# Attention outputs turned in 32x32 blocks by VectorE, with `w_in`'s rows loaded to match; batch 0's first layer in four parts of 128 tokens; four column tiles to a PSUM bank

## The chip, the core and the metric

The kernel runs on one core of a Trainium2 chip. Its engines are TensorE (PE, with its weight loads shown apart as PEld), VectorE (DVE), ScalarE (ACT), GpSimd (POOL, which also issues the DMAs that convert types) and SyncE (SP, which here only issues DMAs). The metric is the device time of one execution in microseconds. Before the change it is 340.51 us, the median of three runs (339.76 to 341.34).

## What is computed

Eight batches of global-local attention with 8 heads of 64: 32 global queries attend to all 544 keys, and 512 local queries attend to the 32 global keys and to the local keys at most 32 positions away. The 8 x 544 rows of 512 outputs then go through two layers with a gate between them. Inputs and output are float32; the kernel computes in float16 and sums in float32.

```python
s_g = scale * np.matmul(q_g, k_all.transpose(0, 1, 3, 2))
out_g = np.matmul(sm(s_g), v_all)
s_ll = np.where(np.abs(pos[:, None] - pos[None, :]) <= 32, scale * np.matmul(q_l, k_l.transpose(0, 1, 3, 2)), -1e9)
s_l = np.concatenate([scale * np.matmul(q_l, k_g.transpose(0, 1, 3, 2)), s_ll], axis=-1)
out_l = np.matmul(sm(s_l), np.concatenate([v_g, v_l], axis=2))
x = concatenate([out_g, out_l], axis=2).transpose(0, 2, 1, 3).reshape(8 * 544, 512)
h = x @ w_in                     # 512 -> 2048
g = h * np.clip(h + 3, 0, 6) / 6
out = g @ w_out                  # 2048 -> 512
```

## The kernel before, in words

**Order of work.** The program is not written in the order in which it runs. Each step is an `Op` with its engine (or a choice of two), an expected cost, the steps it depends on, the buffers it takes and the buffers it reads. The steps stand in streams (`s` scores, `mx` mask and maximum, `ex` exponentials, `t` turned probabilities, `av` values, `nm` normalisation, `xp` turned outputs, `mf` first layer, `t1` and `gate` its gate, `ms` second layer, and so on), each stream with a rank. `Plan.lay` (L118) picks the next step again and again: the one that can start first by its own clock, and within 0.03 us of that the one with the lowest rank. Costs, ranks and the constants `SPARE` and `ALONE` of `Plan` therefore decide the order on each engine, and that order is then fixed: each engine runs its instructions in it, waiting for what they need. `SPARE` is what DVE's finish must be ahead of ACT's for a copy that either may do. `ALONE` decides whether PE may enter an operation on part of its array when only one such operation is ready.

**Local attention** (`local`, L603). The 512 local tokens of a batch are 16 blocks of 32. Step `n` of four handles a pair of blocks `2n`, `2n+1` of each half of the sequence (`f` is the half). Scores (L624 for batches 2 to 7, L637 for batches 0 and 1, which arrive as 32-bit words) go to PSUM tiles `s`, for half of batch 0's pairs to `m`; DVE adds the mask and takes the maximum (L664); ACT takes the exponential (L670); PE turns the eight 128x128 blocks of probabilities (L679) into the PSUM tile `t`; ACT or DVE copies them to `et` (L308 and L310, the two sides of `either`, L303); PE multiplies by the values (L693, 64 small matmuls into the tile `a`); DVE takes the reciprocal of the sums and normalises to `x` (L701, L702). Then four PE matmuls with the identity turn `x` (L715), again into `t` (for batch 0 into `t` or `m`), and ACT or DVE copies the result to `xt` (stream `xpc`), where a partition is one of 128 rows of `w_in`.

**Global attention** (`globe`, L723) does the same in two steps `s` of four heads each: scores (L735, L743), maximum (L751 for each half, L752), exponentials (L757, L758), turning (L768), values (L777), normalisation (L785, L786); after the second, PE turns both (L792) and a copy puts them into `xg`, which collects the global rows of all batches.

**Layers.** `first` (L813) makes one column tile of 128 of the 2048 hidden columns: four matmuls over the 512 inputs (L821) into one PSUM tile `m` of three, then ACT makes `t1` (L833) and DVE the gate (L828), which writes `gts`. `moe_first` (L868) calls it for 16 column tiles; for batch 0 twice, each time for half of the tokens. `second` (L838) makes 128 rows of the output: 16 matmuls (L850), a copy to `ot` (L858 or L860) and a store from SP. `moe_global` (L891) does both layers for the 256 global rows. The first layer of a batch needs `xt` of all its pairs (of batch 0's half, of its two pairs). The scores of batch `b` are held until the first layer of batch `b-1` has come to a set point (`hold`).

**Loads.** POOL issues all loads from the inputs in a fixed order: batch 0's `q`, `k`, `v`, then eight loads of `w_in` (L505, a quarter of the rows by half of the columns, at most three under way), batch 1, four loads of `w_out` (L513), then the later batches. SP copies `rawq`, `rawk` and `vg` within the chip's memory for later batches and issues the stores. Batch 0 handles its pairs in the order 1, 0, 2, 3.

Of the kernel before, what the change touches and what calls it, by code (L numbers as in the profile page):

```python
# [37 lines left out]
class Plan:  # L38
# [6 lines left out]
    SWITCH, ALONE = 0.097, 0.0  # L45
    SPARE, PHASES = 0.3, 9
# [137 lines left out]
def kernel(  # L184
# [33 lines left out]
    AHEAD = 3  # L218
    HALVES = 1
# [22 lines left out]
    for c in range(NDFF):  # L242
        sizes[f"gts{c}"] = 2
# [34 lines left out]
    gts = [tiles(f"gts{r}_", NDFF, [P, Sl], FP16) for r in range(2)]  # L278

    mps = tiles("m", 3, [P, 512], FP32, pp)  # L280
    sps = tiles("s", 2, [P, 512], FP32, pp)
# [4 lines left out]
    for name, rank in (("l0", 0), ("ld", 5), ("lq", -2), ("sh", 0), ("sq", 0), ("st", 2), ("g0", 0), ("ga", -9), ("first", -9), ("gc", -3), ("msk", 1), ("tq", lambda n: 0 if n < 5 else 3), ("kg", 0.5), ("vs", 1.5), ("clr", 1),  # L286
                       ("s", -1), ("mx", lambda n: 1.2 if n < 33 else 2.7), ("ex", 1.2), ("t", -0.5), ("etc", 0), ("av", 0), ("nm", 0),
                       ("xp", -1.2), ("xpc", 0), ("gx", 1), ("gxc", 1),
                       ("mf", lambda n: 9 + n * 1e-3), ("ms", lambda n: 9 + (n + 2 * NDFF + 2) * 1e-3), ("t1", 0), ("gate", -1.4), ("ot", 1.5)):
        plan.stream(name, rank)  # L290
# [161 lines left out]
    def vg_load(b, to):  # L452

        st = state[b]
        v = st["v"] = Buf("v", NI // 2 + 2)
# [42 lines left out]
    def load_w_in():  # L498
        n = dff // 2
        rows = moe_w_in.rearrange("(k a e d) c -> a k d e c", k=2, a=2, e=2)  # L500
        got = []
        for i in range(2):
            for k in range(2):
                for a in range(2):
                    got.append(load("l0", "POOL", 0.65, 1.4, w_in_t[i][a * D:(a + 1) * D, 2 * k:2 * k + 2],  # L505
                                    rows[a, k, :, :, i * n:(i + 1) * n], got[-AHEAD:][:1] if len(got) >= AHEAD else ()))
# [96 lines left out]
    def local(b, n, spare, halves=False):  # L603
# [8 lines left out]
        def scored(r):  # L612
            return mps[ps[r].slot] if spare else sps[r]
# [69 lines left out]
        def summed(t):  # L683

            return aps[t.slot][:, :, 0:NC * D1].rearrange("p u (c d) -> p u c d", c=NC)

        def values():
            o = summed(av)
            for un, i in enumerate(pair):
                for c in range(NC):  # L690
                    for e in range(2):
                        for f in range(2):
                            nc.tensor.matmul(out=o[quarter(e, f), un, c, 0:D + 1],  # L693
                                             lhsT=ets[et.slot][:, un, c, quarter(e, f) if b >= WORDS else quarter(e ^ (c // 2), f)],
                                             rhs=vs[v.slot][:, i % NU, (i + NI * f) // NU, 2 * c + e, 0:D + 1])
# [281 lines left out]
```

## Time and profile before

| | us |
|---|---|
| median of three runs | 340.51 |
| profiled execution | 340.96 |
| span of its instructions | 339.2 |
| PE busy (share) | 313.6 (92%) |
| DVE busy | 257.0 (76%) |
| ACT busy | 234.1 (69%) |
| POOL busy | 156.2 (46%) |
| granted PE clock, mean | 0.983 |

The profile is of one execution. A row of a group of instructions gives line, engine, operation, output<-input by the names in the program, and the shapes; behind the bar busy time and the mean of one in ns; then the idle time ahead of them and what ended it. A row of the timeline or of the chain of waits begins with the start in us and the length. Instructions of one engine overlap at their ends, so a group that runs without a pause takes less than its count times the mean; what one costs in such a stretch is the distance from start to start.

### The profile page before, as it was taken

What the parts mean: (1) busy time and instruction counts of PE and PEld (TensorE: products, weight loads), DVE (VectorE), ACT (ScalarE), POOL (GpSimd) and SP (SyncE); (2) the same over time, 40 slices, a digit from 0 to 9 for tenths busy, and PEclk for the clock granted to TensorE, in tenths of its full rate; (3) what the DMA queues carried; (4) which work ended last, traced back from release to release, by engine and by line L of the source; (5) the groups of instructions that cost most, each with busy time, mean ns of one, the idle gap of its engine ahead of it and who ended that gap; (6) DMA issues with size and microseconds to landing.
All of it is one profiled execution on the core that took longest, in us unless ns stands there. A gap on an engine that the chain in (4) does not pass through costs nothing.

```text
span 339.2 us, 11248 instructions
## 1 busy us (share of the span) xinstructions
PE 313.6 (92%) x4456; PEld 169.5 (50%) x4456; DVE 257.0 (76%) x952; ACT 234.1 (69%) x576; POOL 156.2 (46%) x195
## 2 busy tenths in 40 slices
PE   0648879899999999999999999999999999999996
PEld 0536656454455455544554555454545544445654
DVE  5887997678988799989998999899969844433310
ACT  4778778555888697679867784799699644443431
POOL 8899589108961982694359258756000000000000
PEclk9976999999999999999999999999999999999999
DMA  8989999979960996999679948991000000010103
GB/s 131 185 154 165 185 227 164 177 204 147 221 124 35 154 206 86 91 153 179 145 99 150 169 90 80 183 174 41 31 33 34 35 32 33 31 60 34 62 34 92
DMA packets 107076, 39.27 MB, mean 116 GB/s; under 512 B 92368, under 2 KB 100816, under 8 KB 107024
## 3 DMA queue, kind: packets, MB, share of 16 engines
q0 software_dynamic: 93536, 17.44, 64.6%
q1 hardware_dynamic: 12912, 20.99, 22.7%
q8 instruction: 35, 0.57, 0.7%
q10 hardware_dynamic: 576, 0.13, 0.2%
q14 instruction: 17, 0.14, 0.1%
HBM read 35.39 MB, written 8.91 MB: 131 GB/s over the span
## 4 chain that ended last, share of the span: by engine, by line
PE 87%; DVE 7%; issue 2%; POOL 1%; ACT 1%; POOLq 0%; ACTq 0%
PE m L850 36%; PE m L821 33%; PE t L679 5%; PE a L693 3%; PE s L624 2%; PE t L715 2%; DVE gts L828 1%; PE t L768 1%; PE s L735 1%; PE s L637 1%; PE a L777 1%; DVE sm L664 1%; POOL wout L298 1%; DVE kt L534 1%; DVE qt L529 1%
## 5 line engine op out<-in xcount | busy, mean ns | idle before, releaser
L850 PE MATMUL m<-wout,gts 128*128 128x512 f16 (+1 forms) x560 | 135.1, 373 | 0.0
L828 DVE SCALAR_TENSOR_TENSOR gts<-t,m 128x512 f16<-128x512 f32 (+1 forms) x160 | 95.2, 602 | 46.1 <-ACT t L833 45.0
L821 PE MATMUL m<-xt,win 128*128 128x512 f16 (+1 forms) x576 | 126.9, 359 | 3.0 <-DVE gts L828 1.9
L833 ACT ACTIVATE t<-m 128x512 f32<-128x512 f32 (+1 forms) x160 | 84.3, 532 | 44.6 <-PE m L821 41.2
L486 POOL COPY vs<-v 32x1056 f32<-32x1056 f32 (+3 forms) x81 | 78.2, 966 | 34.9 <-DMA v<-in_v_l_dram 30.1
L670 ACT ACTIVATE ex<-sm,mx 128x128 f16<-128x128 f32 x256 | 86.1, 394 | 8.4 <-DVE mx L664 7.9
L821 PEld LDWEIGHTS <-win 128*128 128x128 f16 x640 | 59.9, 99 | 54.3 <-issue 4.2
L850 PEld LDWEIGHTS <-gts 128*128 128x128 f16 x560 | 51.1, 98 | 48.5 <-issue 0.7
L664 DVE CUSTOM_DVE_ANT_0 sm<-s,mask 128x128 f32<-128x128 f32 x240 | 56.9, 285 | 5.9 <-PE s L624 2.9
L858 ACT COPY ot<-m 128x512 f32<-128x512 f32 (+1 forms) x34 | 19.5, 573 | 16.9 <-PE m L850 16.2
L298 POOL DMA_DIRECT2D rawq<-in_q_l_dram x12 | 12.6, 1057 | 36.2 <-DMA vs<-vg 16.3
L298 POOL DMA_DIRECT2D v<-in_v_l_dram x32 | 28.2, 905 | 0.0
L702 DVE TENSOR_TENSOR x<-a,rec 128x512 f16<-128x512 f32 x32 | 22.1, 692 | 1.1
L664 DVE DVE_READ_ACCUMULATOR2_ANT mx<- 128x1 f32 x256 | 21.3, 83 | 0.0
L679 PE MATMUL t<-ident,ex 128*128 128x128 f16 x256 | 20.9, 228 | 0.0
L679 PEld LDWEIGHTS <-ex 128*128 128x128 f16 x256 | 17.2, 102 | 5.5 <-issue 0.7
L637 PE MATMUL s<-kt,qt 32*32 32x128 f16 x384 | 7.0, 246 | 12.3 <-DVE kt L542 10.0
L571 DVE STREAM_TRANSPOSE qt<-rawq 128x512 f16<-128x512 f16 x24 | 15.9, 692 | 0.0
L575 DVE STREAM_TRANSPOSE kt<-rawk 128x512 f16<-128x512 f16 x24 | 15.8, 687 | 0.0
L308 ACT COPY et<-t 128x1024 f16<-128x1024 f16 x13 | 13.1, 1010 | 3.5 <-PE t L679 3.4
L637 PEld LDWEIGHTS <-qt 32*32 32x32 f16 x512 | 6.5, 102 | 17.7 <-issue 9.6
L310 DVE COPY et<-t 128x1024 f16<-128x1024 f16 x19 | 13.0, 685 | 3.0 <-PE a L693 2.6
(95 smaller groups left out, 262.7 us busy)
## 6 DMA issues: line engine op xcount, KB each, us to landing
out_dram<-ot SPq DMA_DIRECT2D x31, 256.0 KB, 2.1
vs<-vg SPq DMA_DIRECT2D x32, 132.0 KB, 5.8
v<-in_v_l_dram POOLq DMA_DIRECT2D x32, 128.0 KB, 6.5
rawq<-in_q_l_dram POOLq DMA_DIRECT2D x12, 256.0 KB, 5.8
rawk<-in_k_l_dram POOLq DMA_DIRECT2D x12, 256.0 KB, 7.2
rawq<-rawq SPq DMA_DIRECT2D x12, 254.0 KB, 5.6
rawk<-rawk SPq DMA_DIRECT2D x12, 254.0 KB, 5.7
win<-in_moe_w_in_dram POOLq DMA_DIRECT2D x8, 256.0 KB, 6.2
```

The source lines that it names most:

```text
L298: eng.dma_start(out=o() if callable(o) else o, in_=i() if callable(i) else i)
L486: (nc.gpsimd if op.engine == "POOL" else nc.vector).tensor_copy(out=o(), in_=i())
L637: nc.tensor.matmul(out=scored(r)[quarter(e ^ r, f), z:z + P], lhsT=pairs(qt[k.slot])[rows, c, i * W:(i + 1) * W, bb], rhs=pairs(kt[k.slot] ...
L664: nc.vector.tensor_tensor_reduce(out=sms[sm.slot], in0=scored(c // 2)[:, z:z + P], in1=masks[:, m, :], scale=-scale, scalar=3.0e38, op0=AL ...
L670: nc.scalar.activation(out=exs[ex.slot][:, un, c, :], in_=sms[sm.slot], func=EXP, scale=-1.0, bias=mxs[mx.slot])
L679: nc.tensor.matmul(out=turned(tp)[:, z:z + P], lhsT=exs[ex.slot][:, un, c, :], rhs=ident, is_transpose=True)
L702: nc.vector.tensor_tensor(out=xs[x.slot], in0=o[:, :, :, 0:D], in1=recs[rec.slot].to_broadcast([P, 2, NC, D]), op=ALU.mult)
L821: nc.tensor.matmul(out=o if len(x.shape) == 2 else o.rearrange("p (a c) -> p a c", a=2), lhsT=w_in_t[c // 8][:, m, (c % 8) * P:(c % 8 + 1) ...
L828: nc.vector.scalar_tensor_tensor(out=g, in0=shape(t1s[t1.slot][:, 0:n]), scalar=1.0, in1=shape(mps[ps.slot][:, 0:n]), op0=ALU.min, op1=ALU ...
L833: r = plan.add("t1", Op(("ACT", 0.09 + n * 0.00083), lambda: nc.scalar.activation(out=t1s[t1.slot][:, 0:n], in_=mps[ps.slot][:, 0:n], func ...
L850: nc.tensor.matmul(out=mps[ps.slot][:, 0:n], lhsT=gfn(c), rhs=w_out_t[c // 4][:, c % 4, cols], start=(c == 0), stop=(c == NDFF - 1))
L858: nc.scalar.copy(out=o, in_=i)
```

## The change

- `xturn` is one DVE transpose of `x` for each pair, in 32x32 blocks, straight into `xt`. Such a transpose exchanges partition and column only within a block. So the values are summed in another place: partition `32*(h % 4)` + token, and the free dimension holds half, unit and `h // 4`. After the transpose a partition is `32*(h % 4) + d % 32` and one of four slots is `2*(h // 4) + d // 32`. `load_w_in` loads `w_in`'s rows in that order. The columns of `xt` are now pair, half, unit, token, so 128 output rows are two pieces of 64, stored by two DMAs.
- The global rows go the same way: both steps' values are one `av` step (`globe_values`), one normalisation, one DVE transpose into `xg`. The maximum of both halves is one reduction over a PSUM tile of two banks; the two `s` tiles become one of `[P, 2, 512]`.
- `first` takes several column tiles: their matmuls go to one PSUM tile `m` and have one `t1` and one gate. Batch 0 goes through the first layer in four parts of 128 tokens with four column tiles each, in the order of pairs 1, 0, 2, 3; the global rows in two column tiles of 256. `gts` tiles hold four column tiles.
- Constants and ranks of the planner change: `ALONE` 0.0 to 1.0, `SPARE` 0.3 to 0.6, ranks of `s`, `etc`, `xp`, `vs`, `st`.

```diff
-    SWITCH, ALONE = 0.097, 0.0
-    SPARE, PHASES = 0.3, 9
+    SWITCH, ALONE = 0.097, 1.0
+    SPARE, PHASES = 0.6, 9
...
+    PARTS, CG = 4, 4
...
-    gts = [tiles(f"gts{r}_", NDFF, [P, Sl], FP16) for r in range(2)]
+    gts = [tiles(f"gts{r}_", NDFF // CG, [P, CG, Sl], FP16) for r in range(2)]
...
-    sps = tiles("s", 2, [P, 512], FP32, pp)
+    sps = tiles("s", 1, [P, 2, 512], FP32, pp)[0]
...
-        rows = moe_w_in.rearrange("(k a e d) c -> a k d e c", k=2, a=2, e=2)
+        rows = moe_w_in.rearrange("(k h a d) c -> k a h d c", k=2, h=4, a=2)
...
-                    got.append(load("l0", "POOL", 0.65, 1.4, w_in_t[i][a * D:(a + 1) * D, 2 * k:2 * k + 2],
-                                    rows[a, k, :, :, i * n:(i + 1) * n], got[-AHEAD:][:1] if len(got) >= AHEAD else ()))
+                    got.append(load("l0", "POOL", 0.65, 1.4, w_in_t[i][:, 2 * k + a], rows[k, a, :, :, i * n:(i + 1) * n],
+                                    got[-AHEAD:][:1] if len(got) >= AHEAD else ()))
...
-                            nc.tensor.matmul(out=o[quarter(e, f), un, c, 0:D + 1],
+                            nc.tensor.matmul(out=o[hq * W:(hq + 1) * W, f, 2 * un + kh, 0:D + 1],
...
-            st["xt"] = Buf("xt", NDFF * (2 if b == 0 else 1))
+            st["xt"] = Buf("xt", NDFF * (PARTS if b == 0 else 1))
...
         def xturn():
-            o = turned(xp)[:, 0:4 * P].rearrange("d (k z n q) -> d k z n q", k=2, z=NU, n=2)
-            for un in range(2):
-                for kk in range(2):
-                    nc.tensor.matmul(out=o[:, kk, :, un, :], lhsT=xs[x.slot][:, un, 2 * kk:2 * kk + 2].rearrange("p a d -> p (a d)"),
-                                     rhs=ident, is_transpose=True)
-        a = plan.add("xp", Op(("PE", 0.24), xturn, done, [xp], [x], lat=0.25, n=8))
-        st["xT", n] = either(
-            "xpc", 0.5, 0.36,
-            lambda: xts[xt.slot].rearrange("d k (f t) -> d k f t", f=2)[:, :, :, 2 * n * W:(2 * n + 2) * W],
-            lambda: turned(xp)[:, 0:4 * P].rearrange("d (k f t) -> d k f t", k=KC, f=2), [a], new, [xp])
+
+            nc.vector.transpose(out=xts[xt.slot][:, :, n * P:(n + 1) * P].rearrange("p k (t q) -> p t k q", q=W),
+                                in_=xs[x.slot].rearrange("p f (u k) (a q) -> p (f u) (k a) q", u=2, a=2))
+        st["xT", n] = plan.add("xp", Op(("DVE", 0.7), xturn, done, new, [x]))
...
         def top():
-            for f in range(2):
-                nc.vector.tensor_reduce(out=tops[mx.slot][:, f:f + 1], in_=sps[f][:, 0:N1].rearrange("q (a c) -> q a c", a=1), axis=AX, op=ALU.max)
+            nc.vector.tensor_reduce(out=tops[mx.slot][:, 0:1], in_=sps[:, :, 0:N1], axis=AX, op=ALU.max)
...
+    def globe_values(b):
...
+        a = plan.add("av", Op(("PE", 0.48), lambda: [f(av) for f, _, _ in both], [c for _, c, _ in both] + [st["g4"]] + st["v0"],
+                              [av], [et for _, _, et in both] + [v], lat=0.3, n=80, mode=("tall", "tall")))
...
+        st["xg"] = plan.add("gx", Op(("DVE", 0.22), lambda: nc.vector.transpose(
+            out=xg[:, :, b * Sg:(b + 1) * Sg], in_=xgns[xgn.slot].rearrange("p k (a q) -> p (k a) q", q=W)), [n], (), [xgn]))
...
-    def first(xfn, n, gfn, deps, takes, reads):
+    def first(xfn, n, cs, gfn, deps, takes, reads):
...
+        all_ = n * len(cs)
...
+        a = [paced(Op(("PE", 4 * n * 0.000423 + (0.02 if n < 256 else 0.0)), lambda k=k, c=c: mm(k, c), deps + w_in_l[c // 8], [] if k else [ps], reads, lat=0.25, n=8), n / Sl / NDFF)
+             for k, c in enumerate(cs)]
...
-        parts = 2 if b == 0 else 1
+        parts = PARTS if b == 0 else 1
...
+        for at, h in enumerate((1, 0, 2, 3) if parts == 4 else range(parts)):
+            deps = [st["xT", i] for i in range(h * per, (h + 1) * per)]
...
-        second(lambda c: gts[st["gts"][c].slot][c][:, j * P:(j + 1) * P], lambda c: [st["gts"][c]], lambda c: st["gd"][c],
-               [(out[row:row + P, :], 0, P)], parts)
+        rows = out[b * S + Sg:(b + 1) * S].rearrange("(f r) d -> f r d", f=2)
+        second(lambda c: gts[st["gts"][c // CG].slot][c // CG][:, c % CG, j * P:(j + 1) * P], lambda c: [st["gts"][c // CG]], lambda c: st["gd"][c],
+               [(rows[f, j * P // 2:(j + 1) * P // 2], f * P // 2, P // 2) for f in range(2)], parts)
```

## What was predicted, before the changed kernel had run

> **What bounds the kernel now.** I read the chain of waits first, then stretches of the span engine by engine.
>
> ```profile
> PE 87%; DVE 7%; issue 2%; POOL 1%; ACT 1%; POOLq 0%; ACTq 0%
> PE m L850 36%; PE m L821 33%; PE t L679 5%; PE a L693 3%; PE s L624 2%; PE t L715 2%; DVE gts L828 1%; PE t L768 1%; PE s L735 1%; PE s L637 1%; PE a L777 1%; DVE sm L664 1%; POOL wout L298 1%; DVE kt L534 1%; DVE qt L529 1%
> ...
> 0.00:30.00 30.00, 13.12 (x379) 9.94 (x380) 21.70 (x104) 20.57 (x63) 26.70 (x56) 0.84 1.09 155
> 30.00:55.00 25.00, 20.68 (x419) 15.58 (x423) 22.32 (x84) 19.64 (x58) 19.77 (x23) 0.98 1.52 197
> 55.00:75.00 20.00, 18.84 (x411) 10.61 (x399) 13.58 (x58) 12.45 (x35) 5.79 (x7) 1.00 1.54 180
> 75.00:270.00 195.00, 195.00 (x2873) 98.80 (x2871) 177.42 (x667) 154.45 (x371) 103.95 (x111) 1.00 0.97 117
> 270.00:336.00 66.00, 65.96 (x397) 34.56 (x395) 22.00 (x42) 26.67 (x52) 0.00 (x0) 1.00 0.13 45
> ```
>
> The columns of the stretches are length, then busy us of PE, PE's weight loads, DVE, ACT and POOL, then granted clock, DMA share and GB/s. The reader is to see two regimes. Up to 55 us PE is busy for 33.8 of 55; DVE and ACT, working through batch 0's attention and gates, fill much of the rest. From 75 to 336 PE is never idle. But a busy PE need not be a fast one, so I look at how closely its operations follow each other.
>
> ```profile
> 55.54 0.82 PE L850 MATMUL m<-wout,gts 128*128 128x512 f16 x3
> 74.87 1.89 PE L821 MATMUL m<-xt,win 128*128 128x512 f16 x8
> 100.65 0.39 PE L715 MATMUL t<-ident,x 128*128 128x128 f16 x4
> 100.88 1.89 PE L850 MATMUL m<-wout,gts 128*128 128x512 f16 x8
> 102.70 0.43 PE L735 MATMUL s<-kt,qg 64*32 64x288 f16 x8
> 103.06 0.62 PE L679 MATMUL t<-ident,ex 128*128 128x128 f16 x8
> 103.51 1.89 PE L850 MATMUL m<-wout,gts 128*128 128x512 f16 x8
> ...
> 15.68 0.97 PE t L679 x8
> 53.63 1.31 PE m L821 x12
> 279.80 0.86 PE m L850 x4
> ```
>
> From start to start: eight transposes at 103.06 take 0.45 us, 56 ns each; twelve 256-column matmuls 1.31 us, 109 ns each; four 512-column ones 0.86 us, 216 ns each. Eight 512-column matmuls ahead of a score (100.88 to 102.70) take 1.82 us, 0.09 more than 8 x 0.216: that is the price of entering an operation on part of the array. With these prices over all 4456 matmuls, PE's own work is about 303 us. Compared with the start of each matmul, 31.5 us had been lost by 74.87, and only another 1.1 by PE's last matmul. So behind 75 us a microsecond of PE work removed is a microsecond of the end, as long as its feeders keep up. Ahead of 55 us PE work is nearly free, and what counts is when the second layer (L850) of batch 0 can begin.
>
> **The change, part by part.** *1. Turned outputs leave PE.*
>
> ```profile
> L715 PE MATMUL t<-ident,x 128*128 128x128 f16 x120 | 11.6, 219 | 0.4 <-DVE x L702 0.3
> L715 PE MATMUL m<-ident,x 128*128 128x128 f16 x8 | 1.2, 307 | 2.2 <-DVE x L702 2.2
> L792 PE MATMUL t<-ident,xgn 128*128 128x128 f16 x8 | 1.8, 222 | 0.0
> L571 DVE STREAM_TRANSPOSE qt<-rawq 128x512 f16<-128x512 f16 x24 | 15.9, 692 | 0.0
> L529 DVE STREAM_TRANSPOSE qt<-wout 128x512 f32<-128x512 f32 x2 | 2.2, 1080 | 1.6 <-DMA wout<-in_q_l_dram 1.6
> L310 DVE COPY et<-t 128x1024 f16<-128x1024 f16 x19 | 13.0, 685 | 3.0 <-PE a L693 2.6 <-PE t L679 0.2
> L310 DVE COPY xt<-t 128x512 f16<-128x512 f16 x11 | 4.6, 423 | 3.0 <-PE t L715 2.9
> L308 ACT COPY et<-t 128x1024 f16<-128x1024 f16 x13 | 13.1, 1010 | 3.5 <-PE t L679 3.4
> L308 ACT COPY xt<-t 128x512 f16<-128x512 f16 x19 | 11.1, 582 | 6.2 <-PE t L715 6.1
> ```
>
> Gone are 128 + 8 matmuls of 56 ns: 7.6 us. The instruction order of the changed kernel also enters partial-array operations 60 times rather than 76 (the planner now keeps a lone one back): 16 x 0.09 = 1.5 us. The new batch-0 form, priced below, adds 0.3. PE's work falls by 8.8 us.
>
> On DVE come 32 transposes of 512 fp16 columns and 8 small ones. Their source is contiguous, their output runs of 32 at four strides, a form the trace lacks. Bounds: 0.69 us (L571) and 1.08 (L529, twice the bytes); I take 0.69, the row with the same type and count: 22 us, and some 2 for the small ones. In exchange, the order gives 18 of DVE's 19 `et` copies to ACT (-12.3 us) and drops its 11 `xt` copies (-4.7); merged reductions, normalisations and gates lower it further. On ACT 17 more `et` copies (+17.2) stand against 21 `xt` copies (-12.2) and merged `t1` work. So DVE gains a few microseconds at most.
>
> In the long stretch DVE is busy 177 of 195 us, six batches, 29.6 us in 32.5 each. With four transposes (+2.8, +0.3 for the outputs of the global queries) less 2.25 `et` copies (-1.5) and 1.4 `xt` copies (-0.6) it comes to 30.6 at most, while PE's period falls by about 1.1 to 31.4. The cover is thin, 97% against 91%. Hence a new waiting of PE: between 0 (as now) and 6 us (1 us in each of six batches); I take 2, nearer the row that shows no waiting.
>
> *2. Batch 0's first layer in four parts, four column tiles to a bank.* Matmuls on 128 columns instead of 256: 256 x 0.056 = 14.2 us against 128 x 0.109 = 14.0, so +0.3. The row for 56 ns is L679, the same 128x128 weights and 128 moving columns. The other bound is the same operation early on: eight from 15.68 in 0.97 us, 121 ns, which would be +17. I take 56, as the granted clock of the stretch from 30 to 55 is 0.98. The Trainium skill's "TensorE: Matmul & The Clock Gate" (Back-to-back issue gap) speaks against the change here: pairs of weight load and matmul at 128 columns sustain about 81 ns each. By that page this part would take 20.7 us instead of 14.2 (an estimate); the 56 ns at 103.06, weight loads included, disagree with it.
>
> What the parts may bring is an earlier start. These rows carry the stage:
>
> ```profile
> 29.30 0.42 DVE L828 SCALAR_TENSOR_TENSOR gts<-t,m 128x256 f16<-128x256 f32 x1 [1.12 <-ACT t L833]
> 55.00 1.08 DVE L828 SCALAR_TENSOR_TENSOR gts<-t,m 128x256 f16<-128x256 f32 x3 [0.18 <-ACT t L833]
> 27.14 0.56 ACT L308 COPY xt<-m 128x512 f16<-128x512 f16 x1
> L828 DVE SCALAR_TENSOR_TENSOR gts<-t,m 128x512 f16<-128x512 f32 x112 | 76.2, 682 | 30.4 <-ACT t L833 29.5
> L828 DVE SCALAR_TENSOR_TENSOR gts<-t,m 128x256 f16<-128x256 f32 x48 | 19.0, 416 | 15.8 <-ACT t L833 15.4
> 35.38 0.74 POOL L298 DMA_DIRECT2D wout<-in_moe_w_out_dram x1 [1.62 <-DMA xt<-in_q_l_dram]
> 38.17 1.48 POOL L298 DMA_DIRECT2D wout<-in_moe_w_out_dram x2 [2.05 <-DMA vg<-in_v_g_dram]
> wout<-in_moe_w_out_dram POOLq DMA_DIRECT2D x4, 512.0 KB, 12.8
> ```
>
> Before, the first layer waits for two pairs, the last turned and copied at 27.7; its gates run from 29.3 to 56. After, one pair is enough, and the copy through ACT is gone, so the first matmul can come some 2 us sooner. Thirty-two gates of 0.416 (13.3 us) become 16 of 0.682 (10.9); four transposes (+2.8) replace an `xt` copy. DVE's idle time within 30 to 55 is 2.7 us, and part of it closes. I expect L850 to begin at 50.5, 5 us sooner. Bounds: no sooner than the second quarter of `w_out` lands (35.38 + 12.8 = 48.2; the order puts eight matmuls on the first two quarters first), and no later than now, 55.5. I take the middle, a little to the early side, as the last quarter, landing at about 51.7, is only needed later.
>
> Two of batch 1's groups of scores now stand behind that start instead of ahead of it: 2 x 0.65 us back. From that point on the removed work is 8.8 less batch 0's share (16 + 1 transposes 0.9, its switches 0.6, plus 0.3 regained), 7.4 us.
>
> ```profile
> 54.87 0.74 PE L637 MATMUL s<-kt,qt 32*32 32x128 f16 x64
> ```
>
> *3. `w_in` by 128 partitions.* Eight loads of the same size and the same 2 KB rows in fp16, at the same places of POOL's queue: nothing.
>
> *4. Stores cut in two.* 31 row-block stores become 62, the last two 4.
>
> ```profile
> 61.24 0.38 SPq L298 DMA_DIRECT2D out_dram<-ot x1
> 336.07 0.37 ACT L858 COPY ot<-m 128x256 f32<-128x256 f32 x1 [1.33 <-PE m L850]
> out_dram<-ot SPq DMA_DIRECT2D x2, 128.0 KB, 1.7
> ```
>
> An issue holds SP for 0.38 us. What is queued behind a store there are the copies of `rawq`, `rawk` and `vg` for later batches; they are early by whole batches, as no row behind 75 us shows PE waiting for them. If that cover went, 31 x 0.38 = 12 us of SP's 195 would be at stake, not on one batch. At the end one more issue stands ahead of the last landing: +0.3, bounds 0 and 0.4.
>
> **Sum.** Profiled span 339.2 - 7.4 (PE work behind the start of L850) + 1.3 (scores moved behind it) - 5.0 (its earlier start) + 0.3 (last store) + 2.0 (new waiting) = 330.4 us. The profiled execution took 340.96, 1.8 around its span: 332.2. It lay 0.45 above the median of the runs: 331.7, which I round to 331.5. Its own range, with the bounds of the start (-7.3, 0) and of the waiting (0, 6), not both at their worst: 327 to 337.
>
> **Rivals.** *A: the early start doesn't come.* DVE is busy 22.3 of 25 us in 30 to 55, and the parts are still fed by it. Then the 5.0 falls away: 336.5. For it: DVE has 89% there. Against: gates there cost less, and the first one is sooner.
>
> *B: everything is as early as `w_out` allows, no new waiting:* 7.3 instead of 5.0 and 0 instead of 2.0: 327.2. Against it: DVE at 97%.
>
> *C, slower: ACT's queue holds the first layer.* Nearly every pair's `et` copy now stands in ACT's order, 1.01 us that first waits for PE's transposes; behind it is `t1`, behind `t1` the gate, and PE has three banks, some 1.7 us of cover (two column tiles of 0.86). If each of the 28 pairs of batches 1 to 7 costs PE more than (340.5 - 329.7) / 28 = 0.39 us, the kernel is slower than before; at 0.5 us it ends at 343.7. For it: ACT already waits 3.4 us for L679. Against: ACT is busy 154 of 195 us, and hardly more after.
>
> *D: thin matmuls.* If a pair at 128 columns needs more than 56 ns in that stage, say 88, between its two rows, 256 of them take 8.3 us more and L850 begins that much later: 340.0. For it: the clock granted in the first 30 us is only 0.84, and a later release would do this. Against it: the row at 103.06. The Trainium skill's rule of 81 ns, named above, points the same way.
>
> That the change doesn't do what it says is ruled out by the order: no PE transposes of `x` are left.
>
> **Chances.** Forecast 0.58, A 0.20, B 0.09, C 0.09, D 0.04. The range takes in A, B and most of the waiting: 326.5 to 337.5; C and D stay out. One run tells about 0.5%, 1.7 us, from no change. Faster by more: forecast, A and B, less a hundredth for waiting beyond its bound: 0.86. Within: D and the mild end of C, 0.06. Slower: the rest of C, 0.08.
>
> **What would show it.** Right: PE's rows hold no transposes from `x`, the stretch of 195 us is shorter by about 6 and still without PE idle; L850 first appears near 50; transposes to `xt` take about 0.69 us. Wrong: a first L850 at 55 (A), PE idle for gates or for `t1` in the long stretch (DVE or C), 128-column matmuls spaced above 56 ns (D). The forecast fails above all if DVE at 97% makes PE wait.

## The result and the profile after

| | before | after |
|---|---|---|
| median of the runs, us | 340.84 (20 runs, 339.23 to 342.04) | 339.3 (20 runs, 337.62 to 344.98) |
| ratio, 95% interval | | 0.9951 [0.9935, 0.9968] |
| profiled execution, us (span) | 340.96 (339.2) | 341.28 (339.5) |

The kernel became faster by 0.5%, 1.5 us. 331.5 was forecast, and the measured time lies outside the range of 326.5 to 337.5. One of the 20 runs after, 344.98 us, counts as slow and is not in the ratio. The profiled execution of after lies 2.0 us above the median of its runs. So in what follows the traces say where time goes, and the medians say how much.

First the chain of waits of after, then its stretches (columns as in the prediction).

```profile
PE 71%; DMA 13%; issue 6%; POOL 6%; DVE 2%; ACT 1%; POOLq 0%; DVEq 0%; ACTq 0%
PE m L847 31%; PE m L820 29%; DMA rawk<-in_k_l_dram 5%; DMA qtmp<-in_k_l_dram 4%; PE t L680 3%; DMA v<-in_v_l_dram 3%; PE a L697 3%; PE s L625 2%; POOL wout L299 1%; POOL vs L487 1%; PE s L734 1%; PE t L765 1%; POOL win L299 1%; DMA vg<-in_v_g_dram 1%; POOL v L299 1%
```

```profile
0.00:30.00 30.00, 11.72 (x377) 9.38 (x378) 20.33 (x101) 18.64 (x58) 27.63 (x57) 0.84 1.13 145
30.00:55.00 25.00, 20.59 (x448) 18.25 (x447) 20.01 (x48) 17.85 (x35) 17.13 (x20) 0.91 1.45 199
55.00:75.00 20.00, 16.20 (x400) 9.30 (x399) 12.10 (x70) 15.24 (x41) 8.40 (x10) 1.00 1.63 171
75.00:270.00 195.00, 193.23 (x2687) 94.11 (x2686) 173.64 (x613) 153.42 (x348) 104.22 (x111) 0.99 1.04 121
270.00:336.00 66.00, 64.83 (x550) 34.94 (x542) 30.04 (x78) 31.79 (x63) 0.00 (x0) 1.00 0.18 42
```

DMA, which had no share of the chain worth a row before, now has 13% of it, and PE 71% instead of 87%. In 55 to 75 us PE is busy for 16.2 us instead of 18.84, and the long stretch, never idle before, has 1.8 us of idle time. Three rows of the page and one of the page of before show what moved:

```profile
L717 DVE STREAM_TRANSPOSE xt<-x 128x512 f16<-128x512 f16 x32 | 22.4, 701 | 0.1
out_dram<-ot SPq DMA_DIRECT2D x62, 128.0 KB, 2.4
win<-in_moe_w_in_dram POOLq DMA_DIRECT2D x8, 256.0 KB, 10.3
```

```profile
win<-in_moe_w_in_dram POOLq DMA_DIRECT2D x8, 256.0 KB, 6.2
```

The transposes cost what was forecast (0.70 us against 0.69), but a load of `w_in` of the same size lands after 10.3 us instead of 6.2.

The prediction's way of counting is used for all that follows: the start of a PE operation less the work ahead of it at the dense prices is the time lost by then. By this count PE's work fell from 303.2 to 294.5 us, as forecast. The losses (us; the variants are described with the experiments):

| kernel | lost by 75 us | by 120 us | at the last matmul | first layer of batch 2 starts |
|---|---|---|---|---|
| before | 31.5 | 31.8 | 32.6 | 112.8 |
| after | 35.8 | 39.7 | 40.2 | 116.8 |
| x1_win_strips | 32.4 | 35.0 | 35.6 | 113.4 |
| y1_turn_first | 31.1 | 35.7 | 37.5 | 112.7 |
| y3_two_parts | 31.6 | 35.3 | 37.2 | 113.4 |
| z1_batch2_first | 32.6 | 35.0 | 35.6 | 114.2 |
| v1_dve_less_b2 | 32.5 | 36.4 | 37.2 | 113.5 |
| v3_b2_first_less | 32.9 | 34.4 | 34.9 | 113.5 |

Each row is one profiled execution. After loses 7.6 us more than before, 4.3 of them ahead of 75 and 3.6 between there and 120; behind 120 both lose next to nothing. With 8.8 us of work gone and 1.5 more at the tail, that is the whole result of the two profiled executions. Here is PE in after at the second place:

```profile
113.24 0.43 PE L734 MATMUL s<-kt,qg 64*32 64x288 f16 x8
113.94 0.43 PE L697 MATMUL a<-vs,et 128*32 128x65 f16 x32 [0.27 <-ACT et L309]
114.30 0.45 PE L765 MATMUL t<-ident,eg 128*128 128x128 f16 x5
115.94 0.86 PE L765 MATMUL t<-ident,eg 128*128 128x128 f16 x5 [1.19 <-ACT eg L754]
116.84 2.72 PE L820 MATMUL m<-xt,win 128*128 128x512 f16 x6
```

No second-layer matmul (L847) stands between the last steps of batch 2's attention: all 128 of batches 0 and 1 are done, so each step waits for ACT in the open. Before, 124 of 128 were done by then, and no PE wait shows between 75 and 120.

The loss there is not all waiting. The granted clock fell in the same 10 us in after, and not in x1 (stretches of both; the granted clock is third from the end):

```profile
110.00:120.00 10.00, 8.43 (x102) 3.73 (x86) 8.81 (x18) 5.73 (x12) 4.19 (x5) 0.83 0.94 97
```

```profile
110.00:120.00 10.00, 8.27 (x148) 3.92 (x141) 9.42 (x21) 7.24 (x13) 6.44 (x9) 1.00 1.38 121
```

In the trace's clock record that is half the clock for 3.41 us, from 116.2, behind PE's waits of 0.27 and 1.19 us. The eight matmuls on 512 columns from 116.84 took 3.25 us instead of 1.89. So some 1.4 of the 3.9 us that after lost between 75 and 120 are clock. The profiled executions of v1, v2, y1, y2 and z3 have such a stretch of half the clock as well, within 112 to 119 us (v1 and y1 also with 0.83 in the row of 110 to 120); those of before, x1, x4, y3, w1, w2, z1, z2 and v3 have none there. In the table it raises v1 and y1 by about as much. It may be why the times of some variants fall in two groups (v1: 336.25 to 336.38 and 337.93 to 338.45, its profiled execution the longest), but there is one trace for each kernel, so this is not shown.

### The profile page after: what moved, and what is told of

It reads as the page before. It is cut to its first block, busy times and chain, and to the rows that moved or that the text cites. A ratio compares the mean times of both kernels' runs of the same rounds, so it can differ in the third digit from the quotient of the medians.

```text
span 339.5 us, 11130 instructions
## 1 busy us (share of the span) xinstructions
PE 306.6 (90%) x4448; PEld 166.0 (49%) x4448; DVE 256.1 (75%) x905; ACT 236.9 (70%) x542; POOL 157.4 (46%) x196
## 4 chain that ended last, share of the span: by engine, by line
PE 71%; DMA 13%; issue 6%; POOL 6%; DVE 2%; ACT 1%; POOLq 0%; DVEq 0%; ACTq 0%
PE m L847 31%; PE m L820 29%; DMA rawk<-in_k_l_dram 5%; DMA qtmp<-in_k_l_dram 4%; PE t L680 3%; DMA v<-in_v_l_dram 3%; PE a L697 3%; PE s L625 2%; POOL wout L299 1%; POOL vs L487 1%; PE s L734 1%; PE t L765 1%; POOL win L299 1%; DMA vg<-in_v_g_dram 1%; POOL v L299 1%
## 5 line engine op out<-in xcount | busy, mean ns | idle before, releaser
L847 PE MATMUL m<-wout,gts 128*128 128x512 f16 (+1 forms) x560 | 131.2, 374 | 0.0
L820 PE MATMUL m<-xt,win 128*128 128x512 f16 (+1 forms) x704 | 123.6, 328 | 3.1 <-DMA win<-in_moe_w_in_dram 1.4
L827 DVE SCALAR_TENSOR_TENSOR gts<-t,m 128x512 f16<-128x512 f32 x136 | 91.5, 682 | 37.2 <-ACT t L831 36.1
L831 ACT ACTIVATE t<-m 128x512 f32<-128x512 f32 x136 | 80.5, 596 | 44.9 <-PE m L820 42.3
L487 POOL COPY vs<-v 32x1056 f32<-32x1056 f32 (+2 forms) x82 | 78.3, 955 | 36.2 <-DMA v<-in_v_l_dram 32.5
L820 PEld LDWEIGHTS <-win 128*128 128x128 f16 x768 | 64.7, 100 | 56.7 <-issue 5.2
L847 PEld LDWEIGHTS <-gts 128*128 128x128 f16 x560 | 51.3, 98 | 51.0 <-issue 1.7
L309 ACT COPY et<-t 128x1024 f16<-128x1024 f16 x29 | 29.1, 1005 | 5.2 <-PE t L680 4.9
L717 DVE STREAM_TRANSPOSE xt<-x 128x512 f16<-128x512 f16 x32 | 22.4, 701 | 0.1
L697 PE MATMUL a<-vs,et 128*32 128x65 f16 x1024 | 14.8, 198 | 6.1 <-issue 2.8
L697 PEld LDWEIGHTS <-et 128*32 128x32 f16 x1024 | 10.4, 98 | 15.3 <-issue 5.7
L638 PEld LDWEIGHTS <-qt 32*32 32x32 f16 x512 | 6.7, 104 | 19.1 <-issue 10.3
## 6 DMA issues: line engine op xcount, KB each, us to landing
win<-in_moe_w_in_dram POOLq DMA_DIRECT2D x8, 256.0 KB, 10.3
```

What stands on the lines that cost most here:

```text
L309: nc.scalar.copy(out=o(), in_=i())
L487: (nc.gpsimd if op.engine == "POOL" else nc.vector).tensor_copy(out=o(), in_=i())
L697: nc.tensor.matmul(out=o[hq * W:(hq + 1) * W, f, 2 * un + kh, 0:D + 1], lhsT=ets[et.slot][:, un, c, quarter(e, f) if b >= WORDS else quart ...
L717: nc.vector.transpose(out=xts[xt.slot][:, :, n * P:(n + 1) * P].rearrange("p k (t q) -> p t k q", q=W), in_=xs[x.slot].rearrange("p f (u k ...
L820: nc.tensor.matmul(out=mps[ps.slot][:, k * n:(k + 1) * n], lhsT=w_in_t[c // 8][:, m, (c % 8) * P:(c % 8 + 1) * P], rhs=x, start=(m == 0), ...
L827: nc.vector.scalar_tensor_tensor(out=g, in0=shape(t1s[t1.slot][:, 0:all_]), scalar=1.0, in1=shape(mps[ps.slot][:, 0:all_]), op0=ALU.min, o ...
```

## The experiments

Times are medians; ratios are to the kernel before, run next to it on the same chip. Variants of one letter share a chip, except that v1 and v2 ran on another one than v3 and v4; between chips, medians of the kernel before differ by up to 0.6 us. Kernels from x1 on carry line numbers shifted by one in places (L846 is after's L847).

### x1_win_strips: the loads of `w_in` in another shape

```
- rows = moe_w_in.rearrange("(k h a d) c -> k a h d c", k=2, h=4, a=2)
+ rows = moe_w_in.rearrange("(h k d) c -> h d k c", h=4, k=KC)
- for k in range(2):
-     for a in range(2): ... w_in_t[i][:, 2 * k + a] <- rows[k, a, :, :, cols]
+ for h in range(4): ... w_in_t[i][h * W:(h + 1) * W] <- rows[h, :, :, cols]
  # values() and globe(): head h = 2 * hq + kh instead of 4 * kh + hq
```

> The changed kernel with the eight w_in loads in the shape 32 partitions x 4 slots, one plain stride for each, and the heads renumbered to match; everything else stays. Theory T1 (the new shape of the w_in loads is what holds the early stage back: landing 10.3 us instead of 6.2, 3072 more 4-byte packets, w_out and the batch-1 loads 3.3 us later): the loads land in 6 to 7 us again, the last issue of w_out falls from 41.5 to about 38, L847 begins some 3 us before 54.15, and the time falls by 3 us, from 339.3 to about 336. Rival R1 (the early loss comes from the order of work: et copies on ACT, the planner's constants): the loads are quicker but the second layer begins at 54 and the time stays at 339.3, within 0.5.

337.55 us, ratio 0.9897 [0.9869, 0.9926], apart from after's interval. T1 holds, with smaller sizes: 1.75 us in the medians instead of 3, and a second layer that starts 1.0 us sooner instead of 3.

```profile
win<-in_moe_w_in_dram POOLq DMA_DIRECT2D x8, 256.0 KB, 8.6
```

```profile
52.24 1.07 PE L819 MATMUL m<-xt,win 128*128 128x128 f16 x16
53.15 1.03 PE L846 MATMUL m<-wout,gts 128*128 128x512 f16 x4
```

The rows are the page's for the loads and the timeline's for PE. The median landing fell only to 8.6, but the last 2 KB packet of `w_in` ends at 31.65 us (after 35.06, before 32.26), the last issue of `w_out` stands at 38.3 (42.3 in after), and the loss by 75 falls by 3.4 us. The two profiled executions lie 4.85 us apart, more than the medians: some 1.4 of that is the clock at 116 us.

### x2_win_alone: the kernel before with that one part of the change

```
- rows = moe_w_in.rearrange("(k a e d) c -> a k d e c", k=2, a=2, e=2)
+ rows = moe_w_in.rearrange("(k h a d) c -> k a h d c", k=2, h=4, a=2)
- w_in_t[i][a * D:(a + 1) * D, 2 * k:2 * k + 2] <- rows[a, k, :, :, cols]
+ w_in_t[i][:, 2 * k + a] <- rows[k, a, :, :, cols]
```

> The kernel before with nothing but the changed kernel's w_in loads (128 partitions, four strips of 32 rows); w_in's rows then stand in another order than its x, so the output is not the layer's, the work is the same. T1: the loads land in about 10 us, the copies of batch 1 come 3 us later, and the time rises by 2 to 3.5 us, 340.8 to about 343.5. R1: the loads are hidden by the attention of batch 0, as the prediction said (nothing): 340.8, within 0.7.

342.19 us, 1.0039 [1.0017, 1.0061]: 1.3 us slower, loads landing after 10.2 us. So the part that the prediction put at nothing costs 1.3 to 1.8 us, from both sides. Counted from the trace's DMA packets, three loads in flight keep 12 packets going at once in this shape (12.1 in after, 11.7 here, 17 to 20 us), against 14.9 before and 15.2 in x1 (16 to 19 us); as the last loads of after run out, at 34.0 and 34.5 us, 5 are going. The trace of x2 is of its fastest run (341.02) and has lost by 75 us what before had, within 0.2; so the 1.3 us stand on the medians alone. Its output is not the layer's, since `x` keeps its old order.

### x3_one_store: 128 rows in one store

```
- [(rows[f, j * P // 2:(j + 1) * P // 2], f * P // 2, P // 2) for f in range(2)]
+ [(rows[:, j * P // 2:(j + 1) * P // 2], 0, P)]
```

> The changed kernel with each row block stored by one DMA of 128 rows again instead of two of 64. T2 (the split stores cost SP twice the issues, and the last landing 1.5 us instead of the 0.3 predicted): the stretch from the start of the last copy to the end of the span falls from 4.3 to about 2.8 us, time 339.3 - 1.5 = 337.8. Rival: the last landing is set by the bytes and not by the number of DMAs: 339.3, within 0.5.

370.77 us, 1.0848 [1.08, 1.0896]: both theories missed. The chain of waits of its page:

```profile
PE 41%; DMA 34%; POOL 9%; DVE 6%; issue 4%; ACT 3%; SPq 0%; POOLq 0%; DVEq 0%; ACTq 0%
PE m L820 18%; DMA rawq<-in_q_l_dram 16%; PE m L847 16%; DMA v<-in_v_l_dram 9%; POOL vs L487 5%; DMA rawq<-rawq 3%; DMA rawk<-rawk 2%; DVE gts L827 2%; DMA win<-in_moe_w_in_dram 2%; PE a L697 2%; PE t L680 2%; DVE sm L665 1%; POOL v L299 1%; DMA vs<-vg 1%; PE t L765 1%
```

A third of the span hangs on DMAs. The store's destination now has an outer dimension of 2, and its 128 packets of 2 KB run two at a time (mean 1.7 to 2.1, some 6 us a store when one runs alone; before, 13 at once in its stores of 0.83 us). The Trainium skill's "DMA: Bandwidth & Descriptors" (Why a DMA increments its semaphore by 16 and not by 1) has the rule: a DMA runs on the largest number of engines up to 16 that divides the slowest dimension of both sides. That gives 2 here and 4 for a load of `w_in` whose source is 4 x 32 rows; the counts above (2, and 12 for three loads) agree with it.

### x4_old_planner: the planner's constants and ranks of before

```
- SWITCH, ALONE = 0.097, 1.0        SPARE, PHASES = 0.6, 9
+ SWITCH, ALONE = 0.097, 0.0        SPARE, PHASES = 0.3, 9
  # ranks st 2.7 -> 2, vs 2.2 -> 1.5, s -1.7 -> -1, etc 1.5 -> 0
```

> The changed kernel with the planner's ranks and switch constants of the kernel before (SPARE 0.3, ALONE 0, the old ranks for stores, v copies, scores and et copies); the changed arithmetic stays. Theory R1: the new constants, which put the et copies on ACT and keep lone partial-array entries back, cause the early waiting of PE and the loss at 110 to 120 us: without them the time falls by 3 us or more, to 336 or less, though 16 entries of 0.09 us come back. Rival (T1 and T2 hold the loss, the constants earn their 1.5 us): 339.3 + 1.5 = about 341, or more where DVE, with the et copies back on it, holds PE up.

340.68 us, 0.9994 [0.9972, 1.0017]. R1 falls: the new constants earn about 1.4 us, though the two intervals nearly touch. The profiled execution, 338.52, is the fastest of its twelve, so its trace is not set against after's.

### y1_turn_first and y3_two_parts: the start of the second layer

```
# y1, on x1
- ("tq", lambda n: 0 if n < 5 else 3)
+ ("tq", lambda n: 0 if n < 5 else -2 if n < 8 else 3)
# y3, on x1
- PARTS, CG = 4, 4
+ PARTS, CG = 2, 4
```

> x1_win_strips with one rank changed: the turning of batch 1's queries and keys (DVE) goes ahead of the gates of batch 0 instead of between them (in DVE's order after 3 and 5 gates instead of 6, 9 and 12). Theory T3 (in the changed order 240 of batch 0's 256 first-layer matmuls and their gates stand ahead of batch 1's first scores, 80 of 128 before; so the attention of batches 1 and 2 runs 5 to 8 us later than before the change, and the second layer's reserve gives out at 110 to 120 us, where PE loses 2 to 4 us): batch 1's first scores start at 48 or earlier instead of 51.6, batch 2's at 87 instead of 90, the loss in 110 to 120 falls below 1 us, and the time falls by about 1.5 us from x1_win_strips, to 336. Rival (what is gained there is lost again at the start of the second layer, which comes as much later as the turning takes, 4 us): 337.5, within 0.7, or more.

338.05 us, 0.9929 [0.9899, 0.996]. Batch 1's first scores start at 45.0, as T3 wanted, and the loss by 75 is 31.1; but batch 2's start at 89.9 as in x1, and the gain is lost again by 150; some 1.4 us of that is the half clock from 112.3, which x1's profiled execution did not have. T3 falls in its second half: batch 2's scores don't hang on batch 1's attention.

> x1_win_strips with batch 0's first layer in two parts of 256 columns instead of four of 128 (two column tiles to a bank, so the gates and t1 work on 512 columns as in the four parts). The prediction's step (four parts let the second layer start 5 us earlier): the second layer then starts some 3 us later than 53.1 and the time rises by about 3 us, to 340.5. Rival A of the prediction (the parts bring nothing, since DVE feeds both at the same rate): second layer at 53 to 54, time 337.5 within 0.7.

338.55 us, 0.9948 [0.9923, 0.9973]: about 1 us more than x1, with intervals that touch. But its second layer starts at 50.67, sooner than x1's 53.15, not later. By 75 us it had lost 0.8 us less than x1, and behind 120 it lost 1.3 more. What the four parts bring is small, and the start of the second layer does not measure it.

### y2_two_queues: the last stores

```
- load("st", "SP", ...)
+ load("st", "ACT" if parts == 2 and at else "SP", ...)    # at: which of the pair
```

> x1_win_strips with the second of each pair of stores of the very last row block issued by ACT instead of SP, all else alike. T2 (at the end SP issues four 64-row stores in a row at 0.5 to 0.6 us each, and the last landing waits for them: tail behind the start of the last copy 4.4 us against 3.1 before the change): the tail falls by two issues, 1.0 to 1.2 us, to 3.3, and the time by as much, from 337.55 to 336.5. Rival (the landing of the last bytes sets the end): tail and time within 0.4 of x1_win_strips.

337.8 us, 0.9898 [0.9861, 0.9935]; by the time alone inconclusive. In the trace the end comes 3.58 us behind the start of the last copy, 4.38 in x1, 4.64 in after, 3.10 before. The last issues, from the timelines of before, after and y2:

```profile
336.47 0.35 SPq L298 DMA_DIRECT2D out_dram<-ot  x1
```

```profile
336.54 0.59 SPq L299 DMA_DIRECT2D out_dram<-ot  x1
```

```profile
334.00 0.50 ACTq L299 DMA_DIRECT2D out_dram<-ot  x1
```

The last store of 64 rows holds its queue for 0.59 us, where the last one of 128 rows took 0.35; the forecast had taken 0.38 for either. With ACT's queue helping, the last issue starts 0.03 us after the last copy's end (333.60 + 0.37), not 1.3 (after: 334.86 + 0.37 to 336.54).

### w1, w2, v1, v2: more and less work on DVE

On x1, the transposes of one batch's queries done twice (w1: batch 2, w2: batch 5), or three of four left out (v1: batch 2, v2: batches 2 to 7):

```
# turn_q in w1 and w2
+ for _ in range(2 if b == 2 else 1):      # w2: b == 5
      nc.vector.transpose(out=heads(qt...)..., in_=tokens(rawq)...)
# turn_q in v1 and v2
+ if h0 == 0 or b != 2:                     # v2: h0 == 0
      nc.vector.transpose(out=heads(qt...)..., in_=tokens(rawq)...)
```

> x1_win_strips with the four transposes of batch 2's queries done twice: 4 x 0.65 = 2.6 us more of DVE, all else alike. Theory T5 (from 55 to 113 us DVE's total work sets when batch 2's first layer can start, in the changed kernel as before it, and PE has no second-layer work left to bridge it: the stall moved and kept its size in z1_batch2_first): batch 2's first layer starts 2 to 2.6 us later than 113.4, and the time rises by as much, from 337.55 to about 340. Rival (a chain of waits between the engines, with slack on DVE, sets it): below 0.7 us more.

> x1_win_strips with the four transposes of batch 5's queries done twice: the same 2.6 us of DVE, but where the order keeps 12 second-layer matmuls (2.6 us of PE) in hand at the start of the batch's first layer. T5: hidden, 337.55 within 0.7. If DVE bounds all of the long stretch (97% by the prediction's estimate): 2 us more or so, 339.5.

w1 339.42 us (0.9966 [0.9947, 0.9985]), w2 338.79 (0.9936 [0.9911, 0.9961]): 1.9 and 1.2 us of the 2.6. So the point that was to tell T5 apart failed: batch 5 pays too, though 12 second-layer matmuls are in hand there. They stand elsewhere in PE's written order, and can't be called on: PE waits 1.3 us for ACT ahead of the scores at 177.9 (L734), with second-layer matmuls right behind these scores.

> x1_win_strips with three of the four transposes of batch 2's queries left out, so that batch 2's local attention is computed from old data: 1.95 us less of DVE ahead of batch 2, all else alike. T5 (DVE's work ahead of batch 2's first layer sets its start): the start moves from 113.4 to about 111.5, the loss between 75 and 120 us falls from 2.6 to below 1, and the time from 337.55 to about 335.7. Rival (round trips between the engines set it, DVE is only busy): 337.55 within 0.7.

> The same in batches 2 to 7, whose local attention is then computed from old data: 1.95 us less of DVE in each of six batches. T5: no more than v1_dve_less_b2 gains, 335.7 within 0.7, since PE loses only 0.6 us behind 120 in x1_win_strips. If DVE bounds PE in every batch (w2_dve_more_b5 paid for it in batch 5 as well): several microseconds less than v1, 333 or below.

v1 337.15 us (0.9895 [0.9857, 0.9933]), v2 337.84 (0.9913 [0.9886, 0.9939]): nothing gained that can be told apart. PE's waits of v1 between 75 and 120 us (us in total, times, longest) are those of after:

```profile
PE t L765 <- ACT eg L754: 1.2, 1, 1.2
PE a L697 <- ACT et L309: 0.3, 1, 0.3
```

T5 falls. More work on DVE delays PE, less does not bring it forward: something else holds batch 2 as well.

### z1, z2, z3, v3, v4: PE's order ahead of batch 2

In PE's order batch 2's scores stand behind a long run of batch 1's first layer. PE's rows before the change and in x1:

```profile
81.34 3.62 PE L821 MATMUL m<-xt,win 128*128 128x512 f16 x16
84.89 0.42 PE L624 MATMUL s<-kt,qt 64*32 64x128 f16 x32
85.24 5.48 PE L821 MATMUL m<-xt,win 128*128 128x512 f16 x24
```

```profile
80.18 9.89 PE L819 MATMUL m<-xt,win 128*128 128x512 f16 x44
90.00 0.42 PE L624 MATMUL s<-kt,qt 64*32 64x128 f16 x32
```

```
# z1, on x1; z2 = z1 with y2's change
- ("tq", lambda n: 0 if n < 5 else 3)
+ ("tq", lambda n: 0 if n < 5 else 3 if n < 8 else -2 if n < 18 else 3)
# z3, on x1
- SPARE, PHASES = 0.6, 9
+ SPARE, PHASES = 0.3, 9
# v3: z1, and in turn_k
+ if h0 == 0 or b != 2:
      nc.vector.transpose(out=line..., in_=tokens(rawk)...)
# v4: z2, and
- LATE = (2.0, 4.0, 7.0) + ...
+ LATE = (2.0, 4.0, 4.0) + ...
```

> x1_win_strips with one rank changed: the turning of batch 2's queries and keys (DVE) goes ahead of the gates of batch 1, which it stands between otherwise; in PE's order batch 2's first scores then come after 288 first-layer matmuls instead of 316. Theory T4 (the loss at 110 to 120 us is the wait for batch 2's attention: its keys are turned late, between gates, so its scores start at 90.0 against 84.9 before the change, its last xt is done at 113.4, and by then all 128 second-layer matmuls of batches 0 and 1 are used up, 124 before): the scores start at 84 to 85.5, the last xt is done by 110.5, PE loses less than 1 us between 110 and 120, and the time falls by about 2 us, from 337.55 to 335.5. Rival (DVE is short in the whole stretch from 75 to 113: 41 us of instructions in 39 us; who goes first does not matter): last xt at 112.5 to 114, time within 0.7 of 337.55.

337.04 us, 0.9875 [0.9845, 0.9906]. The scores start at 86.3, and the loss between 110 and 120 is gone, but as much is now lost at 82. The wait of PE between 75 and 120, and its rows there:

```profile
PE m L819 <- DVE gts L826: 2.2, 1, 2.2
```

```profile
84.45 1.89 PE L819 MATMUL m<-xt,win 128*128 128x512 f16 x8 [2.18 <-DVE gts L826]
86.27 0.42 PE L624 MATMUL s<-kt,qt 64*32 64x128 f16 x32
```

The four transposes of the keys, 2.48 us in a row, hold up the gates that free PE's banks. The stall has moved. DVE's row:

```profile
80.96 2.48 DVE L575 STREAM_TRANSPOSE kt<-rawk 128x512 f16<-128x512 f16 x4
```

> z1_batch2_first with three of the four transposes of batch 2's keys left out (its local attention is then computed from old data). Theory T6 (two things hold batch 2 at 113 us, either alone enough: in PE's written order its scores stand behind 316 first-layer matmuls, so that the chain behind them ends when the second-layer reserve is gone; and where they are put earlier, the transposes of its keys, 2.5 us in a row, hold up the gates and PE's banks): with the order repaired and the transposes taken away, PE's stall of 2.6 us at 82 falls below 1, and batch 2's first layer starts at 112.5 or earlier instead of 114.2; time 337.04 - 1.7 = 335.3. Rival (neither: the round trips of batch 2's attention): 337.0 within 0.7, with the loss back at 110 to 120.

335.44 us, 0.9837 [0.9807, 0.9867], as T6 had it. With PE's order repaired and three of those transposes gone, the wait is 0.4 us, the scores start at 84.78, and 2.1 us of x1's time are gone. Each alone had gained nothing that can be told apart (z1, and v1 with the queries' transposes). The start of batch 2's first layer missed (113.5, 112.5 expected), though its last `xt` is there at 112.4 (113.4 in x1) and PE does not wait for it: 1.5 us are still lost between 75 and 120, 2.4 in z1. T6 is not shown in full: v3's interval overlaps z1's, and no run leaves out the keys' transposes in x1's order.

```profile
82.96 1.89 PE L820 MATMUL m<-xt,win 128*128 128x512 f16 x8 [0.40 <-DVE gts L827]
84.78 0.42 PE L625 MATMUL s<-kt,qt 64*32 64x128 f16 x32
```

> z1_batch2_first together with the last row block's second stores issued by ACT: all the repairs in one kernel. If T4 and T2 hold, 335.5 - 0.8 = 334.7, which would be 1.8% below the kernel before. If the rival of T4 holds, about 337.

336.51 us, 0.9861 [0.983, 0.9892]. It is the fastest version that leaves nothing out: 1.4% below the kernel before, 0.9% below the changed one (0.9861 / 0.9951). The tail's part in it, 0.5 us, is within the spread.

> x1_win_strips with the planner's preference for ACT back at 0.3: 14 instead of 3 of the copies of the turned probabilities go to DVE. Rival C of the prediction (ACT's queue holds t1 and the gates because the copies wait there for PE): the time falls by 1 us or more, to 336.5. The prediction's view (DVE has the thin cover, ACT has room): 337.55 to 339.

339.85 us, 0.9952 [0.9923, 0.9981], 2.3 us more than x1, with intervals that touch. The copies are not better off on DVE; how much of the 2.3 us is theirs is open, for the profiled execution also had 3.41 us of half the clock, from 113.6.

> z2_batch2_two_queues with the planner told that batch 2's copies of queries and keys land 3 us sooner (4 instead of 7): SP's order then has the first copies of rawk ahead of a pair of stores, DVE's order has all eight transposes of batch 2 ahead of the first gate of batch 1 (they stand behind three gates otherwise), and PE keeps 12 second-layer matmuls for the start of batch 2's first layer (none otherwise). T6: PE loses less than 1.5 us between 75 and 120 (2.4 in z2_batch2_two_queues), time 336.5 - 1.5 = 335. Rival (DVE stands still there for the copies instead, since they land when they land): 336.5 within 0.7.

343.04 us, 1.0056 [1.0034, 1.0077]. Worse than the rival had it. The waits of PE and of DVE between 55 and 120 us:

```profile
PE m L819 <- DVE xt L716: 5.5, 1, 5.5
```

```profile
DVE qg L578 <- DMA gn<-gn: 3.2, 1, 3.2
```

DVE's written order now has the transposes of batch 2 ahead of the last turned outputs of batch 1; it stands still for a copy (`gn`) that SP issues late, and PE waits 5.5 us for `xt`; half the granted clock for 6.83 us follows, from 82.0. The planner's guess at the landing had been the truer one.

## Why the prediction was wrong, step by step

- **PE's work, -8.8 us: right.** 303.2 to 294.5, by the number of operations at the forecast's own prices. Behind the start of batch 2's first layer it shows in full: from there to the last matmul before took 223.0 us (335.76 - 112.77), x1 216.5 (329.96 - 113.43). Of the 8.8 the forecast put 7.4 behind the start of the second layer; its own terms, 8.8 - 0.9 - 0.6 + 0.3, give 7.6.
- **Transposes at 0.69 us, DVE's cover: price right, cover too thin in the estimate.** 0.70 measured; DVE was busy 173.6 of the 195 us, 89%, not 97%. What counted was the place of its work: 2.5 us in a row in front of a gate is more than the banks cover.
- **Matmuls on 128 columns at 56 ns (against rival D): right for most.** In after 16 of them stand between 53.25 and 54.15 us, 56 ns each. Of the 256, 29 took 100 to 120 ns, in the two stretches of half the granted clock (20.6 to 30.9 and 34.3 to 37.7 us). The late ones:

```profile
49.81 2.84 PE L820 MATMUL m<-xt,win 128*128 128x128 f16 x48 [1.33 <-DVE gts L827]
52.58 0.74 PE L638 MATMUL s<-kt,qt 32*32 32x128 f16 x64
53.25 1.07 PE L820 MATMUL m<-xt,win 128*128 128x128 f16 x16
54.15 1.89 PE L847 MATMUL m<-wout,gts 128*128 128x512 f16 x8
```

- **"`w_in` by 128 partitions. Eight loads of the same size ... nothing": wrong, 1.3 to 1.8 us.** Size and row length were compared, the shape was not: 4 x 32 rows instead of 64 in the outer dimensions. The loads land later and push back `w_out` and batch 1's data behind them in POOL's queue (x1, x2).
- **"I expect L850 to begin at 50.5, 5 us sooner": wrong; this is the step that failed most.** It began at 54.15. Even without the loads' cost it is 53.15 (x1), and the loss by 75 is 32.4, above the 31.5 of before. The step also took the start of the second layer for the measure, and it isn't: two parts start it at 50.67 and are 1 us slower (y3). The first layer did begin 1.9 us sooner, as forecast (25.85 against 27.75). What then held it, as far as the traces go, is two things; what a start without them would gain, no run shows. First, PE waits at 31 to 34 us for copies that now stand on ACT, rival C's mechanism, here in batch 0; before has no such wait there, and x1 has the same two (2.0 and 0.6). From the waits of PE in after ahead of 75 us:

```profile
PE a L697 <- ACT et L309: 1.9, 1, 1.9
PE a L697 <- ACT vs L485: 0.6, 1, 0.6
```

  Second, from 37.6 to 53 us DVE is busy for 14.78 of 15.40 us in x1 (14.26 before): its 16 gates of 0.68 us stand between the transposes that batch 1 needs (its scores start at 51.6 in x1, 45.5 before). This is rival A. y1, which let these transposes go first, lost by 150 what it had gained by 75. z3 has no wait for `et` there, and its second layer starts only 0.45 us sooner than x1's (52.70), though it ran at half the clock for longer (to 38.5 us, x1 to 36.3).
- **"Behind 75 us a microsecond of PE work removed is a microsecond of the end, as long as its feeders keep up": the condition failed for batch 2.** Whatever PE saved ahead of 113 us met a batch 2 whose last `xt` comes at 112.0 to 113.5 in before, x1, v1 and z1 alike (116.8 in after). Two things hold it there, as far as v3 shows it: PE's written order, with its scores behind 44 first-layer matmuls, and the transposes in front of the gates. That is 2.1 us between the medians of x1 and v3, and 1.1 between their fastest runs (336.43 and 335.31). The +2.0 put down for new waiting was meant for DVE's cover in six batches; what came is 2.6 us in x1, most of it at batch 2 and for ACT, and 3.9 in after, of which some 1.4 are clock. That the sizes lie near is luck.
- **Last store, +0.3, bounds 0 to 0.4: mis-sized.** The tail grew by 1.5 us. One more issue was counted at 0.38; there are two more, and each of the four takes 0.48 to 0.60.
- **Rival C (copies on ACT): against the measurement in the long stretch.** Copies back on DVE do not make the kernel faster (z3). In batch 0 its wait is there, as said above.

Where the forecast's span of 330.4 us and the measured 339.5 part can be read by the same count. The forecast comes to 29.2 us lost by 75 (31.5 - 5.0 for the early start + 1.3 for the moved scores + 1.4 of removed work that lies ahead of that start), 3.1 behind it (1.1 + 2.0), and 0.3 more at the tail. After lost 35.8 and 4.4, and has 1.5 more at the tail. So of the 9.1 us, 6.6 arose ahead of 75, 1.3 behind it (about the size of the half clock) and 1.2 at the tail. Of the 6.6, 3.4 go with the shape of the loads (x1), and 3.2 stay for the early start that did not come. In the medians, where the miss is 7.8, the loads are 1.3 to 1.8; the 2.1 of v3 are no further part of it, since 2.0 of waiting were in the forecast. Why no variant has lost less than 31.1 us by 75 stays open; no run here takes DVE work away there. v3 leaves work out, so its 2.1 us are what a repair could gain at most.

## What to carry to other kernels

Here, work taken off the busiest engine counted only behind the last point where that engine waited for others; look for the point where its reserve of ready work is used up, for ahead of it a written order decides, not the sum of the work. A load or store of the same bytes and row length is the same only if its outer dimensions are; compare those first. When a stall may have two causes, undoing one can move it, so test them together before dropping either. And before two traces are compared, look at the granted clock in both: here a wait of 1.2 us was followed by 1.4 us of slower matmuls in one execution and by none in another.

## What the runs showed of the hardware

- The outer dimension of a DMA goes with how many of its packets run at once: 2 with an outer 2 (31.5 us on this kernel, x3 against after), about 12 for three loads with an outer 4 (after, x2), 15 for three loads with 64 or 32 (before, x1).
- A store holds SP's queue for longer by its shape: typically 0.47 to 0.60 us for 64 rows (after), 0.33 to 0.38 for 128 rows (before), and 0.51 to 0.58 for 128 rows as 2 x 64 (x3). So it is not the number of rows alone.
- Waits of PE of 0.3 and 1.2 us at 110 to 116 us were followed by 3.41 us of half the granted clock in the profiled executions of after and v1, and not in those of x1 and w1, which have the same waits. Eight matmuls on 512 columns then took 3.25 us in after instead of 1.89 in x1: some 1.4 us of its profiled time that not every execution pays.
